# Fused attention and feed-forward: the feed-forward step regrouped from 256 tokens x 256 inner units to 512 tokens x 128 inner units, with the order of all engines written out

## The chip, the cores and the metric

The kernel runs on one core of a Trainium2 chip. The metric is the time of one execution in device microseconds (us); smaller is better. A profiled execution has a span as well, from the first to the last recorded instruction, which is a little shorter than its time.

## The reference

Two parts run one behind the other. The first is a sparse attention over 4 batches x 8 heads x 768 tokens x 64 dimensions. Each query sees the 31 keys nearest to it and 24 summaries, one for each block of 32 keys; a key summary is a maximum over its block, a value summary a mean:

```python
k_sum = k.reshape(B, H, nb, block, D).max(axis=3)
v_sum = v.reshape(B, H, nb, block, D).mean(axis=3)
mask_l = np.abs(pos[:, None] - pos[None, :]) < window
scores_s = scale * np.einsum('bhsd,bhnd->bhsn', q, k_sum) + np.log(block)
scores_all = np.concatenate([np.where(mask_l, scores_l, -1e9), scores_s], axis=-1)
a = softmax(scores_all)
x = np.matmul(a, np.concatenate([v, v_sum], axis=2))
```

The second is a feed-forward layer on the 3072 tokens x 512 channels that result, with 2048 inner units and the function Mish between two matrix products:

```python
h = x @ w_in
g = h * np.tanh(np.log1p(np.exp(h)))
out = g @ w_out
```

The two weight matrices are held as 64-bit floating-point numbers.

## The kernel before

**Work and tiles.** The 3072 tokens are cut into 12 chunks of 256 (c = 0 to 11), three to a batch. A chunk's attention has four units, one for each pair of heads (hp). A unit goes through: `att_load` (DMAs of queries with keys `qk` and of values `vw`; for a new batch also all keys `ks`, whose block maxima `km` DVE takes, and all values `vsum`, whose block sums `vq` DVE takes and whose means go back through a small DMA `vm<-vq` and from there into `vw<-vm`); `att_scores` (matmuls `sc` on PE, four masked row minima on DVE, line 261, four exponentials on ACT, line 266, the reciprocal of the sum on DVE, the scaling of `pr` on POOL, line 271); `att_transpose` (`pt_ps` on PE, copy `pt` on ACT); `att_values` (`x_ps` on PE, then the split of the result into a rounded part `xh` on ACT and a rest `xl` on DVE).

**Two-part numbers.** PE multiplies in a rounded 32-bit format, so each factor is split into a high and a low part and each product is made of three matmuls: high by high, low by high, high by low.

**Feed-forward.** The 2048 inner units are 16 blocks of 128 (fc). A step of `ff_in` takes one chunk and two blocks: 2 blocks x 4 channel blocks x 3 = 24 matmuls with 256 columns (line 313) into one bank `ph`. `ff_act` makes Mish on ACT (line 321), the high part `gh` (ACT for the first two chunks, DVE behind them, line 325) and the low part `gl` on DVE (line 326). `ff_out` adds the step into two output tiles `po` with 12 matmuls of 512 columns (line 340), two steps later. Eight steps make a chunk, 96 steps the kernel.

**Weights.** There are 32 weight blocks of 128 x 512 numbers, 16 of `w_in` and 16 of `w_out`. `load_weight` brings one in by a DMA of 512 KB into one of three staging buffers and converts it: two integer operations on DVE (lines 116, 117), a scaled copy on ACT (119), a clamp and a merge on DVE (120, 122), the high part by ACT (124), the low part by POOL (125). The converted blocks stay for the whole run.

**Order.** The list of steps runs chunks 0 and 1 beside each other, chunk 1 four steps behind. A dictionary `at` gives the turns at which the attention units of later chunks are put in. The program is then handed to a scheduler that works from a model of the times and sets the order on each engine anew; so the order on an engine isn't the one written. Each engine, and SP's queue of DMA issues, runs its own list strictly in that order and waits on semaphores.

Of the kernel before, what the change touches and what calls it, by code (L numbers as in the profile page):

```python
# [20 lines left out]
P = 128  # L21
# [15 lines left out]
NP_ = NFC // 2  # L37
EARLY = 10
NR = (S - CH) // P
LEAD = 4  # L40
AHEAD = 3
# [14 lines left out]
def fused_kernel(ctx: ExitStack, tc: tile.TileContext, q0, qk, kt, v0, vw, vs, w_in, w_out, out):  # L56
# [5 lines left out]
    xp = ctx.enter_context(tc.tile_pool(name="xp", bufs=3))  # L62
# [44 lines left out]
    def load_weight(src, hi, lo, name):  # L107
        t = stage.tile([P, WP], I64, tag="stage", name=name)
        nc.sync.dma_start(t, src)
        words = t.bitcast(U32).rearrange("p (f two) -> p f two", two=2)  # L110
        low, high = words[:, :, 0], words[:, :, 1]
        f = ff.tile([P, WP], F32, tag="f", name=f"{name}_f", bufs=3)
        x = ff.tile([P, WP], U32, tag="x", name=f"{name}_x", bufs=2)
        u = f.bitcast(U32)

# [3 lines left out]
        nc.scalar.activation(f, high.bitcast(F32), AF.Copy, scale=2.0 ** -OFFSET)  # L119
# [6 lines left out]

    def load_weights(n):
# [4 lines left out]
    weights = [(w, 2 * fp + j) for fp in range(NP_) for w in range(2) for j in range(2)]  # L132

# [101 lines left out]
    def att_psum(c, name):  # L235

        pool, tag = (ps_o, "o") if c == 0 else (ps_a, "a")
        return pool.tile([P, 512], F32, tag=tag, name=name)

    def att_scores(c, hp):  # L240
# [24 lines left out]
        for s in range(NQ):  # L265
            nc.scalar.activation(pr[:, s, :], pr[:, s, :], AF.Exp, scale=-1.0, bias=nm[:, s:s + 1],  # L266
                                 accum_out=sm[:, s:s + 1])
        rs = small.tile([P, NQ], F32, tag="rs", name=f"rs{c}_{hp}")
        nc.vector.tensor_scalar_add(rs, sm, 1e-9)
        nc.vector.reciprocal(rs, rs)  # L270
        nc.gpsimd.tensor_mul(pr, pr, rs.unsqueeze(2).broadcast_to([P, NQ, KA]))  # L271
        u["p"] = pr

    def att_transpose(c, hp):
        u = units[c, hp]
        ps = att_psum(c, f"pt_ps{c}_{hp}")
# [6 lines left out]
    def att_values(c, hp):  # L283
        u = units.pop((c, hp))
        if c not in xs:
            xs[c] = (xp.tile([P, HP, CH], F32R, tag="xh", name=f"xh{c}"),
                     xp.tile([P, HP, CH], F32R, tag="xl", name=f"xl{c}"))
        xh, xl = xs[c]
# [7 lines left out]
        nc.scalar.copy(xh[:, hp, :], ps[:, :CH])  # L296
        nc.vector.tensor_sub(xl[:, hp, :], ps[:, :CH], xh[:, hp, :].bitcast(F32))  # L297
# [5 lines left out]
    def ff_in(c, fp):  # L303
        i = c, fp
        xh, xl = xs[c]

        pool, tag = (ps_a, "a") if c == NCH - 1 and fp in (NP_ - 1, NP_ - 3) else (ps_h, "h")
        ph = pool.tile([P, 2, CH], F32, tag=tag, name=f"ph{c}_{fp}")
        for j in range(2):
            wh, wl = (weight(0, part, 2 * fp + j) for part in range(2))  # L310
            for cc in range(NCC):
                for n, (w, x) in enumerate(((wh, xh), (wh, xl), (wl, xh))):
                    nc.tensor.matmul(ph[:, j, :], w[:, cc * P:(cc + 1) * P], x[:, cc, :],  # L313
                                     start=(cc == 0 and n == 0), stop=(cc == NCC - 1 and n == 2))
        st[i] = {"h": ph.rearrange("p j t -> p (j t)")}

    def ff_act(c, fp):

        s = st[c, fp]
        g = ff.tile([P, 2 * CH], F32, tag="g", name=f"g{c}_{fp}", bufs=3)  # L320
        nc.scalar.activation(g, s["h"], AF.Mish)  # L321
        gh = ff.tile([P, 2 * CH], F32R, tag="gh", name=f"gh{c}_{fp}", bufs=3)
        gl = ff.tile([P, 2 * CH], F32R, tag="gl", name=f"gl{c}_{fp}", bufs=3)

        (nc.scalar.copy if c < 2 else nc.vector.tensor_copy)(gh, g)  # L325
        nc.vector.tensor_sub(gl, g, gh.bitcast(F32))  # L326
        s["g"] = (gh, gl)

    def ff_out(c, fp):
        i = c, fp  # L330
        gh, gl = st.pop(i)["g"]
        if fp == 0:
            po[c] = [ps_o.tile([P, DM], F32, tag="o", name=f"po{c}_{t}") for t in range(CH // P)]
        for t in range(CH // P):
            for j in range(2):
                fc = 2 * fp + j
                tok = slice(j * CH + t * P, j * CH + (t + 1) * P)
                wh, wl = (weight(1, part, fc) for part in range(2))
                for n, (g, w) in enumerate(((gh, wh), (gl, wh), (gh, wl))):
                    nc.tensor.matmul(po[c][t], g[:, tok], w,  # L340
                                     start=(fc == 0 and n == 0), stop=(fc == NFC - 1 and n == 2))
        if fp == NP_ - 1:
            for t in range(CH // P):
                o = ff.tile([P, DM], F32, tag="o", name=f"o{c}_{t}")
                nc.scalar.copy(o, po[c][t])
                nc.sync.dma_start(out[c * CH + t * P:c * CH + (t + 1) * P, :], o)


    todo = [(c, hp) for c in range(NCH) for hp in range(HP)]

    steps = [(c, i - c * LEAD) for i in range(NP_ + LEAD) for c in range(2) if 0 <= i - c * LEAD < NP_]
    steps += [(c, fp) for c in range(2, NCH) for fp in range(NP_)]

# [22 lines left out]
    def turn(k, lag):  # L376

        return k + lag - (k >= len(steps) - AHEAD)

# [64 lines left out]
```

## Time and profile before

| what | value |
|---|---|
| median of 3 runs | 713.33 us (710.31 to 714.52) |
| the profiled execution: time | 712.24 us |
| its span | 710.5 us |
| mean granted PE clock | 0.976 |
| PE busy | 672.8 us, 95% |
| ACT busy | 354.2 us, 50% |
| DVE busy | 301.1 us, 42% |
| POOL busy | 111.5 us, 16% |

Matmuls overlap one another, so the mean length of one says little; what counts is the distance from one start to the next. On DVE and ACT, too, an instruction starts a little (about 0.08 us) before its forerunner's recorded end. In rows of the timeline the columns are: start in us, length in us, engine, line, operation, output<-inputs, shapes, count, and in brackets how long the engine had stood idle and what ended that.

### The profile page before, as it was taken

To read this page: it belongs to the slowest core of one execution; us is meant where nothing else is said; L and a number is where in the kernel's file an instruction comes from. 1 tells how busy PE (TensorE), PEld (TensorE's weight loads), DVE (VectorE), ACT (ScalarE), POOL (GpSimd) and SP (SyncE) were. 2 spreads that over 40 slices of the span, in tenths; PEclk is the share of its full clock that TensorE was granted. 3 is DMA by queue.
4 is the path that set the end of the run, shared out by engine and by line. 5 is a ranking of instruction groups with operands and counts; after the bars stand their busy time and mean duration, and the time that the engine had idled before them with its cause. 6 is when DMAs were issued, how large, how long until landed. Compare 5 with 4: busy or idle time off the path is not lost.

```text
span 710.5 us, 12644 instructions
## 1 busy us (share of the span) xinstructions
PE 672.8 (95%) x4960; PEld 603.6 (85%) x4960; DVE 301.1 (42%) x872; ACT 354.2 (50%) x776; POOL 111.5 (16%) x151
## 2 busy tenths in 40 slices
PE   4978788799999999999999999999999999999998
PEld 3767677688898998998998998998998998998996
DVE  4899989952322334443223233222222322322211
ACT  2767755544556644644644644644644644644110
POOL 3454554301010010010100100100100100010000
PEclk9969899899999999999999999999999999999999
DMA  9876655772221323531311311311311311300000
GB/s 276 239 235 204 184 171 155 216 230 88 88 71 44 111 56 104 161 89 43 116 43 43 116 43 44 117 44 43 116 43 43 117 43 44 115 15 1 30 1 30
DMA packets 30683, 70.56 MB, mean 99 GB/s; under 512 B 4768, under 2 KB 9504, under 8 KB 30624
## 3 DMA queue, kind: packets, MB, share of 16 engines
q1 hardware_dynamic: 30624, 69.76, 32.2%
q8 instruction: 39, 0.64, 0.4%
q14 instruction: 20, 0.16, 0.1%
HBM read 61.15 MB, written 6.29 MB: 95 GB/s over the span
## 4 chain that ended last, share of the span: by engine, by line
PE 79%; DVE 11%; DMA 4%; issue 2%; ACT 2%; SPq 0%; POOL 0%; DVEq 0%; POOLq 0%
PE ph L313 34%; PE po L340 33%; PE sc L246 6%; PE x_ps L295 3%; DVE w_x L116 3%; PE pt_ps L278 2%; DVE w_x L117 2%; DVE w_f L122 2%; DMA ks<-kt 1%; DMA vsum<-vs 1%; DMA vw<-vw 1%; DVE w_f L120 1%; ACT pr L266 1%; DVE gl L326 1%; DVE vq L196 1%
## 5 line engine op out<-in xcount | busy, mean ns | idle before, releaser
L313 PE MATMUL ph<-xh,w_early_in_hi 128*128 128x256 f32 x480 | 138.7, 291 | 3.2 <-ACT w_early_in_hi L124 2.4
L313 PE MATMUL ph<-xh,w_early_in_lo 128*128 128x256 f32 x480 | 139.1, 291 | 2.2 <-POOL w_early_in_lo L125 2.2
L313 PE MATMUL ph<-xl,w_early_in_hi 128*128 128x256 f32 x480 | 138.9, 290 | 1.2 <-DVE xl L297 1.2
L325 DVE CAST gh<-g 128x512 fp32r<-128x512 f32 x80 | 34.3, 429 | 209.3 <-ACT g L321 196.6
L271 POOL TENSOR_TENSOR pr<-pr,rs 128x480 f32<-128x480 f32 x48 | 49.0, 1021 | 348.2 <-DVE rs L270 309.7
L313 PEld LDWEIGHTS ph<-xh,w_early_in_hi 128*128 128x128 f32 x480 | 93.9, 196 | 7.1 <-ACT w_early_in_hi L124 3.2
L313 PEld LDWEIGHTS ph<-xl,w_early_in_hi 128*128 128x128 f32 x480 | 93.8, 196 | 3.9 <-DVE xl L297 1.7
L313 PEld LDWEIGHTS ph<-xh,w_early_in_lo 128*128 128x128 f32 x480 | 93.9, 196 | 3.2 <-POOL w_early_in_lo L125 2.6
L340 PE MATMUL po<-w_early_out_hi,gh 128*128 128x512 f32 x240 | 94.3, 396 | 2.5 <-ACT gh L325 2.5
L340 PE MATMUL po<-w_early_out_hi,gl 128*128 128x512 f32 x240 | 95.6, 398 | 0.0
L340 PE MATMUL po<-w_early_out_lo,gh 128*128 128x512 f32 x240 | 95.0, 396 | 0.0
L321 ACT ACTIVATE g<-ph 128x512 f32<-128x512 f32 x96 | 57.4, 598 | 67.0 <-PE ph L313 66.5
L313 PE MATMUL ph<-xh,w_late_in_hi 128*128 128x256 f32 x288 | 82.5, 287 | 0.1
L313 PE MATMUL ph<-xh,w_late_in_lo 128*128 128x256 f32 x288 | 81.9, 284 | 0.1
L313 PE MATMUL ph<-xl,w_late_in_hi 128*128 128x256 f32 x288 | 81.1, 282 | 0.0
L266 ACT ACTIVATE pr<-pr,nm 128x120 f32<-128x120 f32 x192 | 73.7, 385 | 5.8 <-DVE nm L261 5.3
L321 ACT ACT_TABLE_LOAD x44 | 56.5, 1283 | 38.7 <-PE ph L313 38.3
L326 DVE TENSOR_TENSOR gl<-g,gh 128x512 fp32r<-128x512 f32 x96 | 70.7, 736 | 8.1 <-ACT gh L325 5.5
L296 ACT CAST xh<-x_ps 128x256 fp32r<-128x256 f32 x48 | 17.9, 372 | 100.7 <-PE x_ps L295 100.7
L280 ACT COPY pt<-pt_ps 120x512 f32<-120x512 f32 x48 | 28.1, 586 | 71.9 <-PE pt_ps L278 71.5
L266 ACT ACT_TABLE_LOAD x43 | 55.2, 1283 | 8.4 <-DVE nm L261 7.8
L340 PE MATMUL po<-w_late_out_hi,gl 128*128 128x512 f32 x144 | 56.7, 394 | 1.6 <-DVE gl L326 1.6
(75 smaller groups left out, 1149.9 us busy)
## 6 DMA issues: line engine op xcount, KB each, us to landing
qk<-qk SPq DMA_DIRECT2D x44, 496.0 KB
vw<-vw SPq DMA_DIRECT2D x48, 192.0 KB
w<-w_in SPq DMA_DIRECT2D x16, 512.0 KB
w<-w_out SPq DMA_DIRECT2D x16, 512.0 KB
ks<-kt SPq DMA_DIRECT2D x16, 384.0 KB
out<-o SPq DMA_DIRECT2D x24, 256.0 KB
vsum<-vs SPq DMA_DIRECT2D x12, 384.0 KB
vw<-vm SPq DMA_DIRECT2D x44, 48.0 KB
```

Of the source, the lines that this page charges most:

```text
L116: nc.vector.tensor_scalar(out=x, in0=low, scalar1=29, scalar2=None, op0=ALU.logical_shift_right)
L246: nc.tensor.matmul(ps[:, s * KA:(s + 1) * KA], u["qk"][:, s, 0:P], u["qk"][:, s, P:], start=True, stop=True)
L266: nc.scalar.activation(pr[:, s, :], pr[:, s, :], AF.Exp, scale=-1.0, bias=nm[:, s:s + 1], accum_out=sm[:, s:s + 1])
L271: nc.gpsimd.tensor_mul(pr, pr, rs.unsqueeze(2).broadcast_to([P, NQ, KA]))
L280: nc.scalar.copy(pt.rearrange("p s q -> p (s q)"), ps[:KA, :])
L295: nc.tensor.matmul(x, u["v"][:, s, d], pt, start=True, stop=True)
L296: nc.scalar.copy(xh[:, hp, :], ps[:, :CH])
L313: nc.tensor.matmul(ph[:, j, :], w[:, cc * P:(cc + 1) * P], x[:, cc, :], start=(cc == 0 and n == 0), stop=(cc == NCC - 1 and n == 2))
L321: nc.scalar.activation(g, s["h"], AF.Mish)
L325: (nc.scalar.copy if c < 2 else nc.vector.tensor_copy)(gh, g)
L326: nc.vector.tensor_sub(gl, g, gh.bitcast(F32))
L340: nc.tensor.matmul(po[c][t], g[:, tok], w, start=(fc == 0 and n == 0), stop=(fc == NFC - 1 and n == 2))
```

## The change

**Feed-forward steps.** Two chunks make a group g of 512 tokens. A step is now a group with one block of 128 inner units: `ff_in` 4 x 3 = 12 matmuls of 512 columns, `ff_out` 4 output tiles x 3 = 12 matmuls of 512 columns. There are 6 groups x 16 = 96 steps. The first step needs the attention of both chunks 0 and 1 (all channels, 512 tokens). The high part is now `ah`, the low part `al`, made in `ff_split`.

**Order.** Up to the first step the scheduler still sets the order, from a longer written list. From the first step on, everything stands within `tc.manual_schedule()`, and each engine takes the order in which the loop writes it. Within turn i that order is: `ff_in(i)`, Mish of i, values of the unit of turn i-2, scores of this turn's unit with the DMAs of keys, the DMAs of values, two weight blocks, the split of i, the sums of this turn's unit, `ff_out(i-2)`, the transposes of the unit of turn i-1. Chunks 2 and 3 have their eight units at turns 6 to 13, one each; later groups have one unit at every second turn.

**Weights in two halves.** `load_weight` begins a block (DMA, ACT's scaled copy, DVE's lines 117 and 118); `finish_weight` does the rest (126, 128, 130 on ACT, 131 on POOL) while the next block has been begun. Ten blocks are begun ahead of the first step, two at each of turns 0 to 10. Blocks come one `w_out`, one `w_in` in turn.

**Buffers.** Mish outputs, both halves of a weight and the outputs share one tag with 6 buffers; x has 2 instead of 3.

```diff
-NP_ = NFC // 2
+CG = 2
+TG = CG * CH
+NG = NCH // CG
-LEAD = 4
-AHEAD = 3
-    ff = ctx.enter_context(tc.tile_pool(name="ff", bufs=2))
+    ff = ctx.enter_context(tc.tile_pool(name="ff", bufs=6))
...
     def load_weights(n):
-        for w, fc in weights[:n]:
-            load_weight((w_in, w_out)[w][fc], weight(w, 0, fc), weight(w, 1, fc), f"w{w}_{fc}")
-        del weights[:n]
+        for _ in range(n):
+            if weights:
+                begun.append(load_weight(*weights.pop(0)))
+            if len(begun) > 1 or not weights and begun:
+                finish_weight(*begun.pop(0))
...
+    def ff_in(g, fc):
+        xh, xl = xs[g]
+        ph = ps_h.tile([P, TG], F32, tag="h", name=f"ph{g}_{fc}")
+        wh, wl = (weight(0, part, fc) for part in range(2))
+        for cc in range(NCC):
+            for n, (w, x) in enumerate(((wh, xh), (wh, xl), (wl, xh))):
+                nc.tensor.matmul(ph, w[:, cc * P:(cc + 1) * P], x[:, cc, :],
+                                 start=(cc == 0 and n == 0), stop=(cc == NCC - 1 and n == 2))
...
+        (nc.scalar.copy if g == 0 else nc.vector.tensor_copy)(ah, a)
+        nc.vector.tensor_sub(al, a, ah.bitcast(F32))
...
+    begin_with("K0 K1 S0 K2 V0 S1 W1 T0 K3 V1 S2 A0 T1 V2 S3 W1 A1 T2 V3 A2 T3 l0 W1 A3")
...
+    begin_with("l1 s0 W2 t0 s1 l2 W1 a0 t1 s2 W2 l3 a1 t2 s3 W1 a2 t3 l4 W1 a3 k5 v5")
...
+        at[(g - 1) * NFC + (2 * u - 1 if g > 1 else NFC - CG * HP - 2 + u)] = c, hp
...
+    with tc.manual_schedule():
+        for i in range(len(steps) + 2):
+            if i < len(steps):
+                ff_in(*steps[i])
+                ff_act(*steps[i])
+            if i - 2 in at:
+                att_values(*at[i - 2])
+            if i in at:
+                att_scores(*at[i])
+                if unit := next(keys, None):
+                    att_load_keys(*unit)
+            if i - 2 in at and (unit := next(values, None)):
+                att_load_values(*unit)
+            load_weights(2)
+            if i < len(steps):
+                ff_split(*steps[i])
+            if i in at:
+                att_normalize(*at[i])
+            if i >= 2:
+                ff_out(*steps[i - 2])
+            if i - 1 in at:
+                att_transpose(*at[i - 1])
```

**Three places of the new order.** A name such as w1_12 is block 12 of matrix 1 (`w_out`; matrix 0 is `w_in`), qk3_0 is pair 0 of chunk 3, al0_1 is group 0, step 1; the last number tells a tile from others.

On DVE, before, in the middle of the conversions (chunks 0 and 1):

```order
L120 TENSOR_SCALAR w1_11_f_1088<-w1_11_f_1088 128x512
L116 TENSOR_SCALAR w0_12_x_1143<-w0_12_1140 128x512
L122 SCALAR_TENSOR_TENSOR w1_11_f_1088<-w1_11_f_1088,w1_11_x_1089 128x512
L120 TENSOR_SCALAR w0_12_f_1142<-w0_12_f_1142 128x512
L117 SCALAR_TENSOR_TENSOR w0_12_x_1143<-w0_12_1140,w0_12_x_1143 128x512
L116 TENSOR_SCALAR w0_13_x_1154<-w0_13_1151 128x512
L122 SCALAR_TENSOR_TENSOR w0_12_f_1142<-w0_12_f_1142,w0_12_x_1143 128x512
```

On DVE, now, turn 0 from its second block on and the beginning of turn 1:

```order
L117 TENSOR_SCALAR w0_6_x_752<-w0_6_749 128x512
L118 SCALAR_TENSOR_TENSOR w0_6_x_752<-w0_6_749,w0_6_x_752 128x512
L126 TENSOR_SCALAR w1_4_f_740<-w1_4_f_740 128x512
L128 SCALAR_TENSOR_TENSOR w1_4_f_740<-w1_4_f_740,w1_4_x_741 128x512
L344 TENSOR_TENSOR al0_0_737<-a0_0_734,ah0_0_736 128x512
L117 TENSOR_SCALAR w1_5_x_782<-w1_5_779 128x512
L118 SCALAR_TENSOR_TENSOR w1_5_x_782<-w1_5_779,w1_5_x_782 128x512
```

The low part al of a step now stands directly behind the merge (L128) of the turn's second weight block and ahead of everything of the next turn, where before the low part (`gl`) stood wherever the scheduler had put it between conversions.

On ACT a turn now stands as: Mish, scaled copy and high part of one block, scaled copy and high part of the next, then the high part ah. So ah waits, by ACT's order, for the merge of the weight block ahead of it on DVE, and al on DVE for ah.

On SP's queue, before, the last eight weight blocks are issued in one piece:

```order
L109 DMA w0_12_1140<-w_in 128x512
L109 DMA w0_13_1151<-w_in 128x512
L109 DMA w1_12_1231<-w_out 128x512
L109 DMA w1_13_1242<-w_out 128x512
L109 DMA w0_14_1298<-w_in 128x512
L109 DMA w0_15_1309<-w_in 128x512
L109 DMA w1_14_1409<-w_out 128x512
L109 DMA w1_15_1420<-w_out 128x512
```

On SP's queue, now, turn 8:

```order
L222 DMA qk3_0_1228<-qk 128x992
L235 DMA vw2_2_1231<-vw 96x512
L239 DMA vw2_2_1231<-vm0_2_309 24x4x128
L111 DMA w1_12_1234<-w_out 128x512
L111 DMA w0_14_1245<-w_in 128x512
```

On SP's queue, now, turn 10, the last with weights:

```order
L222 DMA qk3_2_1430<-qk 128x992
L205 DMA vsum1_0_1434<-vs 96x1024
L209 DMA vm1_0_1433<-vq1_0_1436 24x4x32
L235 DMA vw3_0_1440<-vw 96x512
L239 DMA vw3_0_1440<-vm1_0_1433 24x4x128
L111 DMA w1_14_1443<-w_out 128x512
L111 DMA w1_15_1454<-w_out 128x512
```

The weight blocks of turns 8 to 10 are now issued behind attention DMAs of the same turn: qk3_0 needs the buffer that this turn's scores (chunk 2, pair 2) read, vw2_2 the buffer that this turn's values read, vm1_0 the result of DVE's sum of this turn.

More of the change, by code (lines that the diff above doesn't have):

```diff
@@ L118, in load_weight, with finish_weight @@
                                        op0=ALU.bitwise_and, op1=ALU.bitwise_or)
-        nc.scalar.activation(f, high.bitcast(F32), AF.Copy, scale=2.0 ** -OFFSET)
+        return w, fc, f, x
+    def finish_weight(w, fc, f, x):
+        u = f.bitcast(U32)
+        hi, lo = (weight(w, part, fc) for part in range(2))
         nc.vector.tensor_scalar(out=f, in0=f, scalar1=-_as_f32(F32_MAX), scalar2=_as_f32(F32_MAX),
@@ L284, in att_values @@
         u = units.pop((c, hp))
[L285 to L288, printed above, removed]
+        g, half = divmod(c, CG)
+        if g not in xs:
+            xs[g] = (xp.tile([P, HP, TG], F32R, tag="xh", name=f"xh{g}"),
+                     xp.tile([P, HP, TG], F32R, tag="xl", name=f"xl{g}"))
+        xh, xl = (x[:, hp, half * CH:(half + 1) * CH] for x in xs[g])
         ps = att_psum(c, f"x_ps{c}_{hp}")
@@ L295, in att_values @@
                 nc.tensor.matmul(x, u["v"][:, s, d], pt, start=True, stop=True)
-        nc.scalar.copy(xh[:, hp, :], ps[:, :CH])
-        nc.vector.tensor_sub(xl[:, hp, :], ps[:, :CH], xh[:, hp, :].bitcast(F32))
+        nc.scalar.copy(xh, ps[:, :CH])
+        nc.vector.tensor_sub(xl, ps[:, :CH], xh.bitcast(F32))
     st = {}
     po = {}
[L303 to L346, printed above, removed]
@@ new lines, in ff_split, with ff_out @@
+    def ff_split(g, fc):
+        a, ah, al = st[g, fc]
+        (nc.scalar.copy if g == 0 else nc.vector.tensor_copy)(ah, a)
+        nc.vector.tensor_sub(al, a, ah.bitcast(F32))
+    def ff_out(g, fc):
+        _, ah, al = st.pop((g, fc))
+        if fc == 0:
+            po[g] = [ps_o.tile([P, DM], F32, tag="o", name=f"po{g}_{t}") for t in range(TG // P)]
+        wh, wl = (weight(1, part, fc) for part in range(2))
+        for t in range(TG // P):
+            tok = slice(t * P, (t + 1) * P)
+            for n, (a, w) in enumerate(((ah, wh), (al, wh), (ah, wl))):
+                nc.tensor.matmul(po[g][t], a[:, tok], w,
+                                 start=(fc == 0 and n == 0), stop=(fc == NFC - 1 and n == 2))
+            if fc == NFC - 1:
+                o = ff.tile([P, DM], F32, tag="t", name=f"o{g}_{t}")
+                (nc.vector.tensor_copy if t % 2 else nc.scalar.copy)(o, po[g][t])
+                nc.sync.dma_start(out[g * TG + t * P:g * TG + (t + 1) * P, :], o)
@@ L376, in turn @@
-    def turn(k, lag):
-        return k + lag - (k >= len(steps) - AHEAD)
-    loaded = HP + 1
-    for i in range(len(steps) + 2):
-        parts = at.get(i, ())
-        now = [x for k, x in enumerate(steps) if turn(k, 0) == i]
-        for x in now:
-            ff_in(*x)
-        for x in now:
-            ff_act(*x)
-        for f, c, hp in parts:
-            if f is not att_transpose:
-                f(c, hp)
-                if f is att_scores and loaded < len(todo):
-                    att_load(*todo[loaded])
-                    loaded += 1
-        load_weights(4 if i < LEAD else 2)
-        if i >= 2:
-            ff_out(*steps[i - 2])
-        for f, c, hp in parts:
-            if f is att_transpose:
-                f(c, hp)
+    for c, hp in todo[CG * HP:]:
+        g, half = divmod(c, CG)
+        u = half * HP + hp
+        at[(g - 1) * NFC + (2 * u - 1 if g > 1 else NFC - CG * HP - 2 + u)] = c, hp
```

59 lines of the change are left out of this document (35 added, 24 removed).

## The prediction

> **What bounds the kernel now.** I read the page first: the span, the slices, the shares of the chain.
>
> ```profile
> span 710.5 us, 12644 instructions
> PE   4978788799999999999999999999999999999998
> DVE  4899989952322334443223233222222322322211
> PEclk9969899899999999999999999999999999999999
> PE 79%; DVE 11%; DMA 4%; issue 2%; ACT 2%; SPq 0%; POOL 0%; DVEq 0%; POOLq 0%
> ```
>
> A slice is 710.5 / 40 = 17.8 us. Up to the eighth (142 us) DVE is mostly at 8 or 9 tenths and PE at 7 or 8; behind the ninth PE is full to the end. So there are two stages: one in which weights are converted, and one in which only matmuls count. The windows and the chain of waits put numbers on both (columns of a window: length, then busy time and instructions of PE, PEld, DVE, ACT, POOL, then PE's clock, DMA share, GB/s).
>
> ```profile
> 40.00:60.00 20.00, 16.82 (x119) 14.81 (x120) 19.49 (x45) 14.16 (x37) 11.86 (x11) 0.68 0.66 212
> 404.17:457.54 53.37, 53.37 (x403) 48.35 (x402) 17.47 (x64) 25.31 (x58) 4.85 (x8) 1.00 0.22 68
> ```
>
> ```profile
> 146.78 3.45 DMA vsum<-vs
> 151.88 6.05 DMA vsum<-vs
> 404.17 2.86 PE ph L313 x24
> 407.03 2.75 PE po L340 x12
> 696.07 10.98 PE po L340 x48
> ```
>
> In the second stage a chunk is 53.37 us of unbroken PE: 8 steps of 2.86 + 2.75 = 5.61, and 53.37 - 44.9 = 8.5 for four attention units, 2.1 each. In the first stage DVE is busy 19.49 of 20 us at 40 to 60. The last long wait that is not PE's is the sum's transfer, ending at 157.9.
>
> **The change: matmuls.** 24 matmuls of 256 columns take 2.86, 12 of 512 take 2.75, so a step of `ff_in` should fall to 2.75: 96 x 0.11 = 10.6 us less PE work in all. The rows are of the same operands' types and the same clock of 1.00. The Trainium skill, "TensorE: Matmul & The Clock Gate", Back-to-back issue gap, gives N / 2.4 + 2.5 ns for one matmul taken alone, which is 109 and 216 ns; the trace's spacing, 119 and 229 ns, is wider at both. By that formula a pair saves only 2.6 ns, and the total below would come out about 7 us higher.
>
> **The change: the way to the first step.** The first step now needs chunks 0 and 1 whole. The listing of the order shows nine merges of weights (L128) and five reciprocals (L287) on DVE up to the one of chunk 1's first unit, and then hardly any conversions beside units 1 to 3. Before, DVE had done as much when this merge, the ninth, had ended:
>
> ```profile
> 51.78 0.68 DVE L122 SCALAR_TENSOR_TENSOR w_f<-w_f,w_x 128x512 uint32<-128x512 uint32 x1
> ```
>
> So 52 us. Behind it stand three units one after the other, since PE's order puts each unit's scores behind the transposes of the one before. The links of that chain:
>
> ```profile
> 25.19 0.65 PE L278 MATMUL pt_ps<-ident,pr 128*120 128x128 f32 x4 [1.18 <-POOL pr L271]
> 34.84 0.69 PE L295 MATMUL x_ps<-pt,vw 120*64 120x64 f32 x16
> 40.95 1.90 PE L246 MATMUL sc<-qk 128*128 128x120 f32 x8
> 402.07 1.15 PE L246 MATMUL sc<-qk 128*128 128x120 f32 x8
> ```
>
> ```profile
> 131.38 0.40 ACT L266 ACTIVATE pr<-pr,nm 128x120 f32<-128x120 f32 x1 [0.92 <-DVE nm L261]
> ...
> 132.81 0.19 ACT L266 ACTIVATION_READ_ACCUMULATOR pr<-pr,nm 128x1 f32 x1
> ```
>
> ```profile
> 26.71 0.99 POOL L271 TENSOR_TENSOR pr<-pr,rs 128x480 f32<-128x480 f32 x1 [1.57 <-DVE rs L270]
> ```
>
> ```profile
> L261 DVE CUSTOM_DVE_ANT_0 pr<-sc,base 128x120 f32<-128x120 f32 x160 | 36.3, 277 | 8.4 <-PE sc L246 8.1 <-issue 0.4
> L296 ACT CAST xh<-x_ps 128x256 fp32r<-128x256 f32 x48 | 17.9, 372 | 100.7 <-PE x_ps L295 100.7
> L280 ACT COPY pt<-pt_ps 120x512 f32<-120x512 f32 x48 | 28.1, 586 | 71.9 <-PE pt_ps L278 71.5
> ```
>
> Scores 1.15 to 1.90 (the clock was 0.68 in that window), first minimum 0.28 and a hand-over, four exponentials 1.6 (131.38 to 133.00), two small sums on DVE 0.4, POOL 1.0, transposes 0.65, hand-overs about 0.4: 5.5 to 6.9 a unit, and I take 6.1. Ahead of them come the first unit's POOL, transposes and copy, 2.8 with hand-overs; behind them the last copy, values, xh and xl, 2.1. So 52 + 2.8 + 3 x 6.1 + 2.1 = 75 us to the first step. Low end 66 (DVE keeps its 19.49 of 20 from the start: 39 us of work in 43, and short units), high end 79 (long units, DVE late).
>
> **The change: turns 0 to 5.** Here each turn converts two blocks and DVE takes al last. The rows are of before, same shapes:
>
> ```profile
> 101.61 0.68 DVE L326 TENSOR_TENSOR gl<-g,gh 128x512 fp32r<-128x512 f32 x1
> 102.21 0.68 DVE L122 SCALAR_TENSOR_TENSOR w_f<-w_f,w_x 128x512 uint32<-128x512 uint32 x1
> 102.81 0.68 DVE L117 SCALAR_TENSOR_TENSOR w_x<-w,w_x 128x512 uint32<-128x512 uint32 x1
> 103.42 0.41 DVE L120 TENSOR_SCALAR w_f<-w_f 128x512 f32<-128x512 f32 x1
> 103.75 1.51 DVE L116 TENSOR_SCALAR w_x<-w 128x512 uint32<-128x512 uint32 x1
> 105.19 0.68 DVE L122 SCALAR_TENSOR_TENSOR w_f<-w_f,w_x 128x512 uint32<-128x512 uint32 x1
> ...
> 116.24 1.78 DVE L326 TENSOR_TENSOR gl<-g,gh 128x512 fp32r<-128x512 f32 x1
> ```
>
> ```profile
> 103.62 1.36 POOL L125 TENSOR_TENSOR w_late_out_lo<-w_f,w_late_out_hi 128x512 fp32r<-128x512 f32 x1 [2.22 <-ACT w_late_out_hi L124]
> 116.12 1.35 POOL L125 TENSOR_TENSOR w_late_out_lo<-w_f,w_late_out_hi 128x512 fp32r<-128x512 f32 x1 [2.22 <-ACT w_late_out_hi L124]
> ```
>
> ```profile
> 80.92 0.62 ACT L124 CAST w_early_in_hi<-w_f 128x512 fp32r<-128x512 f32 x1
> 81.45 0.61 ACT L325 CAST gh<-g 128x512 fp32r<-128x512 f32 x1
> ```
>
> By starts, a long DVE operation takes 0.60 and a short one 0.34, so the four of a block 1.88. One that meets POOL's subtraction takes 1.44 instead of 0.34 (103.75 to 105.19), 1.1 more, so such a block 2.98. In a turn, counted from its second merge: ACT makes that block's high part (0.53 to the next start) and then ah (0.61), so al can start at 1.2; what is queued behind it on DVE is all of the next turn's weight work. POOL meanwhile makes the low part, 0.7 to 2.1, so al ends at 2.6, as in the row at 116.24. The next block ends its four at 4.5, the second, with POOL in its way, at 7.5. PE would need 2.75 + 2.75 = 5.5, so it waits for al. Six turns of 7.5 are 45 us; bounds 6.6 (al clear of POOL, 0.6 instead of 1.4) and 8.5 (both blocks meet POOL), 40 to 51.
>
> **Turns 6 and 7.** Scores add four minima (0.8) to DVE in turn 6, and in turn 7 the sums and POOL's scaling as well (0.4, and 0.7 of POOL in DVE's way): 8.3 + 9.4 = 17.7, bounds 16 to 19.
>
> **Turns 8 and 9.** The transfers decide here. In SP's listing the two weight blocks stand behind `qk`, which needs a buffer that the turn's scores free, and behind `vw`, which needs one that the turn's values free. Before, such a wait was there too, but no weights behind it:
>
> ```profile
> SPq L224 <- PE x_ps L295: 281.1, 33, 12.4
> ```
>
> ```profile
> 139.94 0.81 SPq L198 DMA_DIRECT2D vm<-vq  x1
> ...
> 149.54 0.84 SPq L228 DMA_DIRECT2D vw<-vm  x1
> ```
>
> The values wait for the copy pt, which on ACT stands behind ah of the turn before, and that stands behind that turn's second high part. From ah's end: pt copy 0.6, values to 2.4, scores to 3.45, `qk`, `vw`, and 0.84 for `vw<-vm`, so the first weight block is issued at 5.1 to 5.4. The page has no landing time for 512 KB; the sum's transfer, 384 KB, took 3.45 and 6.05. I take 4.5: the blocks are there at 9.6, where DVE would want the first at 6. Both are converted, 4.5 to 5.4 with merges and high part: 15 us a turn, 30 for two. Bounds 11 (the 3.45, no collision) and 17 (the 6.05, both collide).
>
> **Turn 10** has three waits in a row on SP: `qk` for scores, `vm` for DVE's sum, `vw<-vm` for `vm`; only then the last two blocks. In the row below DVE gets its buffer back from the small transfer at 142.94, 3.0 after the issue at 139.94; the sum itself takes 1.22.
>
> ```profile
> 142.94 1.22 DVE L196 TENSOR_REDUCE vq<-vsum 96x32 f32<-96x1024 f32 x1 [0.85 <-DMA vm<-vq]
> ```
>
> That is 15 + 1.2 + 0.2 for the mean + 3.0 + 0.84 for `vw<-vm` = 20.2, and 1.8, one clean block, for the sum's place in DVE's list: 22. Bounds: 12, if the sum's data were there long before and DVE reaches it early; 27, if `vsum` lands in 6.05 first. **Turn 11** takes 10 (8.2 to 11), the last conversions without new ones, and 3.5 more reach turn 12's scores.
>
> **The rest is PE.** Left then are 86 `ff_out` and 83 `ff_in`, 169 x 2.75 = 464.8, and 34 units' worth of attention, 34 x 2.1 = 71.4: 536.2. The end costs what it costs now, 710.5 - (696.07 + 10.98) = 3.5. The output copies and their transfers lie beside PE but for the last; DVE's share, 17.47 of 53.37, and ACT's leave room there for every order, so buffers and the written order cost nothing; without that room a turn with attention, 7.6, would show it.
>
> **Sum:** 75 + 45 + 17.7 + 30 + 22 + 10 + 3.5 + 536.2 + 3.5 = 742.9, against the span of 710.5. The profiled execution's time was 712.24, 1.7 more than its span: 744.6, so 745 us. That execution stands 1.1 under the median of the three runs, 713.33, well inside their spread of 4.2, so nothing is added for it. All low ends give 66 + 40 + 16 + 22 + 12 + 8.2 + 3.5 + 539.7 + 1.7 = 709, all high ends 79 + 51 + 19 + 34 + 27 + 11 + 3.5 + 539.7 + 1.7 = 766.
>
> One more price lies in ACT's switches between Mish and the exponential:
>
> ```profile
> 52.93 1.28 ACT L321 ACT_TABLE_LOAD   x1
> 54.22 0.60 ACT L321 ACTIVATE g<-ph 128x512 f32<-128x512 f32 x1
> ```
>
> Mish starts 1.29 after the load began: the load and nothing more. The Trainium skill, "ScalarE: Activation LUTs", What ACT_TABLE_LOAD costs, adds about 1.38 us of drain to each switch, which these rows don't show. By it turns 6 to 11, two switches each, would be up to 12 x 1.38 = 17 us longer and the time up to 761.
>
> **Rivals.** *Weights arrive in time.* Turns 8 to 11 then go by their low bounds, near turn 7's 9.4: 11 + 11 + 12 + 8.5 = 42.5 in place of 15 + 15 + 22 + 10 = 62, so 19.5 less: 725 us. For it: three staging buffers, and a transfer of 3.45. Against it: SP's order.
>
> *Conversion keeps up* (the other side, faster). If DVE's turn is no longer than PE's, 5.5 or 7.6 with attention, PE is bound from the first step on: 75 + 96 x 5.5 + 40 x 2.1 + 3.5 + 1.7 = 692 us. It decides at a DVE turn of 5.5: DVE's bare work is 2 x 1.88 + 0.6 = 4.4 without POOL, 4.4 + 2 x 1.1 = 6.6 with both subtractions in its way. For it: before, DVE did run 19.49 of 20 full, and the first stage there had the same work. Against it: al's wait for ah, which no order of other work fills now.
>
> *The losses are all at their low ends*, 709 us, no change. That the change doesn't do what it says is excluded by the listing, in which every engine has the written order from the first step on.
>
> **How the numbers follow.** Forecast, 726 to 766: 0.58. Weights in time, about 725: 0.16. Conversion keeps up, 690 to 705: 0.15. Low ends, within 0.5% of 713.33 (about what a measurement of this kernel can tell from no change; 709.8 to 716.9): 0.06. Over 766: 0.05. Leaving out the last and the fast case, 0.20, the range is 707 to 766. Faster 0.15, same 0.06, slower 0.58 + 0.16 + 0.05 = 0.79.
>
> **What would show it.** In the changed profile: `ff_in` as x12 of 2.75; the first step at 75; starts of al 7.5 apart in turns 0 to 5, each idle for ACT's ah; in turns 8 to 10 DVE's L117 waiting for a DMA of `w`, and SP's queue waiting for PE ahead of weight blocks; sc of turn 12 at 203; PE full behind it. The prediction is wrong if PE is full before 150, or if DVE never waits for `w`.

## The result, and the profile after

The changed kernel takes 771.9 us (median; 771.61 to 773.79) against 713.24 us (710.31 to 714.52): the ratio is 1.083, 95% interval 1.080 to 1.087. The profiled execution has a span of 770.3 us. Slower was forecast, and 745 us with a range to 766; the loss is 58.7 us where 31 were foreseen.

From the page after, the same five lines that were read of before:

```profile
span 770.3 us, 10267 instructions
PE   6636886745499999999899999989999999999997
DVE  4971887644533323244532232354323232221211
PEclk9755899786599999999999999999999999999999
PE 63%; DVE 16%; DMA 14%; ACT 3%; issue 2%; POOL 1%; SPq 1%; POOLq 0%; DVEq 0%
```

A slice is now 19.3 us. PE isn't full before the twelfth slice (212 us; before, the ninth, 142 us), and two dips of one slice stand behind that, at the 20th (366 us) and the 27th (501). DVE is less busy in the first stage than before, not more: nothing has become the bound by being busy. The share of transfers in the chain has gone from 4% to 14%. The low clock figures stand where PE waits; from 240 us on the clock is 1.00, as it was before. Two windows, first the one in which the first step's attention is made, then turns 8 and 9:

```profile
40.00:60.00 20.00, 6.95 (x39) 6.01 (x40) 12.25 (x35) 8.14 (x25) 8.47 (x8) 0.50 0.58 187
160.00:200.00 40.00, 19.58 (x104) 16.12 (x104) 18.48 (x44) 15.29 (x33) 7.07 (x8) 0.71 0.37 121
```

At 40 to 60 DVE had 19.49 of 20 us before and has 12.25 now. At 160 to 200 no engine is busy for half of the time.

From the chain of waits after, the start:

```profile
50.77 0.99 POOL pr L288
...
61.21 3.40 DMA qk<-qk
...
69.16 3.92 DMA qk<-qk
...
78.28 0.35 DVE w_x L117
```

The first unit of chunk 1 is scaled at 50.8 and turn 0 begins at 78. Then turns 0 and 1 (the rows of the second are those of the first, 8.2 us later):

```profile
84.95 1.38 DVE al L344
86.35 0.44 DVE w_x L117
...
88.60 0.44 DVE w_x L117
...
89.76 1.45 DVE w_f L126
...
92.48 0.62 ACT ah L343
93.12 1.37 DVE al L344
```

And the ends of turns 7 to 11, with the weight transfers that turns 8, 9 and 10 waited for:

```profile
143.45 0.26 ACT ah L343
...
148.32 4.29 DMA w<-w_out
...
158.73 0.61 ACT ah L343
...
164.92 6.86 DMA w<-w_out
...
177.89 0.61 ACT ah L343
...
191.46 3.56 DMA w<-w_out
...
201.13 0.61 ACT ah L343
...
213.36 0.52 ACT ah L343
...
215.10 1.09 PE sc L257 x8
```

Behind them PE is full, but for the turns in which a new batch's values come in. The scores of every second turn, with the transfer that stands between them in the chain:

```profile
330.41 1.09 PE sc L257 x8
...
331.93 4.24 DMA vsum<-vs
...
339.14 1.00 POOL pr L288
...
344.22 1.09 PE sc L257 x8
...
345.75 5.08 DMA vsum<-vs
...
358.89 1.10 PE sc L257 x8
...
387.82 1.08 PE sc L257 x8
...
400.97 1.08 PE sc L257 x8
```

The last pair, 13.15 apart, is a clean one. The four such pairs of turns from 330.41 to 387.82 take 57.41 in place of 52.6: 4.8 us lost here, and 5.5 in the same way from 493 to 551.

The terms of the sum against these rows (us; a turn from one ah's end to the next):

| term | forecast | measured |
|---|---|---|
| first step | 75 | 77.9 |
| turns 0 to 5 | 45 | 48 (7.0 for turn 0, then 8.2 each) |
| turns 6 and 7 | 17.7 | 17.8 |
| turns 8 and 9 | 30 | 34.8 (15.6 and 19.2) |
| turn 10 | 22 | 23.2 |
| turn 11 | 10 | 12.1 |
| to the scores of turn 12 | 3.5 | 1.2 |
| the rest with its end | 539.7 | 555.2 |
| span | 742.9 | 770.3 |

### The profile page after: what moved, and what is told of

Its sections match the earlier page's. It is cut to its first block, busy times and chain, and to the rows that moved or that the text cites. A ratio compares the mean times of both kernels' runs of the same rounds, so it can differ in the third digit from the quotient of the medians.

```text
span 770.3 us, 10267 instructions
## 1 busy us (share of the span) xinstructions
PE 674.9 (88%) x3808; PEld 546.0 (71%) x3808; DVE 313.7 (41%) x884; ACT 340.3 (44%) x758; POOL 109.8 (14%) x151
## 4 chain that ended last, share of the span: by engine, by line
PE 63%; DVE 16%; DMA 14%; ACT 3%; issue 2%; POOL 1%; SPq 1%; POOLq 0%; DVEq 0%
PE ph L328 26%; PE po L354 24%; DMA vsum<-vs 7%; PE sc L257 6%; PE x_ps L314 3%; DMA w<-w_out 3%; DVE w_f L126 3%; DVE w_x L118 3%; PE pt_ps L296 3%; DVE w_f L128 3%; DVE w_x L117 2%; DVE al L344 2%; DVE vq L207 2%; POOL pr L288 1%; DMA qk<-qk 1%
## 5 line engine op out<-in xcount | busy, mean ns | idle before, releaser
L335 ACT ACTIVATE a<-ph 128x512 f32<-128x512 f32 x96 | 57.3, 597 | 191.9 <-PE ph L328 191.7
L354 PE MATMUL po<-w_early_out_hi,ah 128*128 128x512 f32 x240 | 98.9, 412 | 4.9 <-ACT ah L343 3.4
L328 PE MATMUL ph<-xh,w_early_in_hi 128*128 128x512 f32 x240 | 98.9, 412 | 3.2 <-ACT xh L315 3.2
L354 PE MATMUL po<-w_early_out_hi,al 128*128 128x512 f32 x240 | 96.3, 401 | 4.4 <-DVE al L344 4.4
L328 PE MATMUL ph<-xl,w_early_in_hi 128*128 128x512 f32 x240 | 96.0, 400 | 0.0
L328 PE MATMUL ph<-xh,w_early_in_lo 128*128 128x512 f32 x240 | 95.9, 400 | 0.0
L354 PE MATMUL po<-w_early_out_lo,ah 128*128 128x512 f32 x240 | 95.5, 398 | 0.0
L344 DVE TENSOR_TENSOR al<-a,ah 128x512 fp32r<-128x512 f32 x96 | 79.7, 830 | 19.0 <-ACT ah L343 16.2
L277 ACT ACTIVATE pr<-pr,nm 128x120 f32<-128x120 f32 x192 | 73.6, 384 | 14.3 <-DVE nm L272 13.8
L335 ACT ACT_TABLE_LOAD x41 | 52.6, 1283 | 32.8 <-issue 19.5
L328 PE MATMUL ph<-xh,w_late_in_hi 128*128 128x512 f32 x144 | 58.1, 404 | 0.0
L354 PE MATMUL po<-w_late_out_hi,ah 128*128 128x512 f32 x144 | 57.9, 402 | 0.0
L354 PEld LDWEIGHTS po<-w_early_out_hi,ah 128*128 128x128 f32 x240 | 46.5, 194 | 15.6 <-ACT ah L343 4.6
```

What stands on the lines that cost most here:

```text
L328: nc.tensor.matmul(ph, w[:, cc * P:(cc + 1) * P], x[:, cc, :], start=(cc == 0 and n == 0), stop=(cc == NCC - 1 and n == 2))
L335: nc.scalar.activation(a, st[g, fc], AF.Mish)
L344: nc.vector.tensor_sub(al, a, ah.bitcast(F32))
L354: nc.tensor.matmul(po[g][t], a[:, tok], w, start=(fc == 0 and n == 0), stop=(fc == NFC - 1 and n == 2))
```

## The experiments

The theory after the result: the time goes into lists that are kept strictly in order, in four places. They are the start that needs two chunks, al behind weights, weights behind attention's transfers on SP, and al, ah and the reciprocal behind the sum of a new batch. The rivals: a slower PE clock; DVE's own work; the new step itself. Each run is set against the kernel before on the same chip (714.2, 713.8, 712.2, 714.1, 714.2 and 713.7 us in the six groups below), and the changed kernel's 771.9 is the base unless another is named. The kernel before differs by 2 us between these groups, so a difference of that size between two runs says little. The first step begins at 76.2 to 80.7 us in the profiled executions of runs that share its start, so a single profile can be some us early or late from the start on.

**1. The sums of a new batch last in the turn, from turn 12 on.**

```diff
-            if i - 2 in at and (unit := next(values, None)):
-                att_load_values(*unit)
+            unit = next(values, None) if i - 2 in at else None
+            if unit and i < LATE:
+                att_load_values(*unit)
             load_weights(2)
...
                 att_normalize(*at[i])
+            if unit and i >= LATE:
+                att_load_values(*unit)
```

> The values' loads with DVE's sum of a new batch (vsum, L207) moved behind the split and the sums of the turn, from turn 12 on; the work is the same. Theory: from turn 12 on the time over the forecast is the wait of DVE for the transfer vsum, ahead of ah, al and the reciprocal: 4.8 us for each of two later batches (scores 13.8, 14.7, 15.0, 13.9 us apart instead of 13.15) and 7.9 us in turns 12 and 13. So 17 us less, 755 us, and no idle time of DVE for vsum on the chain of waits behind 235 us. Rival, a lower PE clock (mean 0.936 against 0.976): no change, 772.

Measured: 762.8 us (757.98 to 764.79), ratio 1.068 [1.064, 1.073]; 9 less, where 17 were expected. From turn 12's scores to the span's end it is 544.7 us in the profile (211.6 to 756.3) against 555.2. The scores between which the changed kernel lost its first 4.8 us:

```profile
325.92 1.08 PE sc L258 x8
...
379.27 1.08 PE sc L258 x8
```

That is 53.35 for four pairs of turns, 52.6 when clean, in place of 57.41. The four pairs from 484.54 to 537.15 take 52.6 in place of 58.1. So the wait for vsum in the later batches was what I took it for, 10 us; the 7.9 for turns 12 and 13 was wrong. From the scores of turn 12 to those of turn 15 this run takes 22.2 us (211.62 to 233.83), and PE is busy for 28.37 of the 28.4 us from 211.6 to 240. The changed kernel took 23.3 there: 1.1 were lost, not 7.9. The clock isn't the cause: it was 1.00 in these stretches in both.

**2. Weight transfers at the head of the turn.**

```diff
         for i in range(len(steps) + 2):
+            for b in weights[:2]:
+                fetched[b] = fetch_weight(*b)
             if i < len(steps):
                 ff_in(*steps[i])
```

> The two weight transfers of a turn issued at its head, ahead of its attention transfers; DVE, ACT and POOL keep their order. Theory: turns 8, 9 and 10 (15.6, 19.2 and 23.2 us from the end of one ah to the next) are long because the transfers stand behind the attention's on SP; ahead of them, turns 8 and 9 fall to 10 or 11, turn 10 to about 17, where the sum stays in the way: 19 us less, 753. Rival, DVE and ACT bound these turns through their own lists: under 5 us less, 767 or more.

Measured: 757.3 us, ratio 1.062 [1.060, 1.064]; 14.6 less. From the chain, the same ends of turns:

```profile
142.53 0.61 ACT ah L349
...
153.93 0.61 ACT ah L349
...
166.04 0.61 ACT ah L349
...
182.39 0.61 ACT ah L349
```

Turns 8, 9 and 10 are 11.4, 12.1 and 16.4 us for 15.6, 19.2 and 23.2. No transfer of weights is left in the chain from 120 to 200 us, and turn 10 waits for vsum (3.48 at 171.47), as expected. Turn 12's scores come 18.4 us earlier (196.65); about 4 of these are given back, since the turns that load a new batch take longer here: 25.2 us for 23.3 from turn 12's scores to turn 15's, and 60.1 for 57.4 over the four pairs of the next batch. Why they do wasn't followed up.

**3. The split ahead of the weights.**

```diff
+            if i < len(steps):
+                ff_split(*steps[i])
             load_weights(2)
-            if i < len(steps):
-                ff_split(*steps[i])
```

> ah and al of a step made ahead of the turn's two weight blocks instead of behind them. Theory: al's wait for ah, which waits for the second merge, is 1.2 us of each 8.2 us turn; without it turns 0 to 5 fall to 6.9, and 6 and 7 by as much: 10 us less, 762. Rival, DVE's own work with POOL in its way fills the turn: turns stay at 7.7 or more, under 4 us less.

Measured: 781.4 us, ratio 1.094 [1.091, 1.098]; 9.5 more. The theory fell as it was put. Turns stayed above 7.7 us, as the rival said, but neither foresaw that the time would rise. The chain of turn 1:

```profile
88.13 0.70 DVE w_f L128
...
88.85 0.62 ACT w_early_out_hi L130
89.47 0.51 ACT a L335
...
90.00 0.63 ACT ah L343
...
90.66 0.03 DVE al L344
...
97.93 0.63 ACT ah L343
```

A turn is 7.93 in place of 8.2. al no longer waits for a merge of its own turn; but on ACT the next Mish now stands behind the high part of the turn before, and ah behind Mish, so that al begins 1.83 us behind the merge's end (88.83 to 90.66) where it had begun 1.19 behind it (91.93 to 93.12). That al no longer meets POOL (0.7 us for 1.37) makes up for this and a little more, 0.3 a turn. The wait went to another list, and in the turns with attention the exponentials stand in it too (in the chain from 143.21, ahead of ah at 144.53): turn 12's scores came at 222.8, not 215.1.

**4. The scheduler throughout.** `with tc.manual_schedule():` becomes `if True:`; steps, halves and buffers are the new ones.

> The new steps, halves and buffers, but the scheduler sets the order of all engines throughout, as in the kernel before. Theory: the loss is the written order, not the new steps: 700 to 740 us, with weights converted by 160 us. Rival, the new step itself costs it, because the first one needs two chunks: the first step not before 70 us and 745 us or more.

Measured: 755.1 us (750.24 to 760.89), ratio 1.059 [1.053, 1.065]. The theory's range is missed, and the figures are those of the rival, 745 us or more with a first step not before 70: steps 0 and 1 are made in pieces beside the attention, and the first 12 matmuls of a step that run on end begin at 85.3. But this run doesn't price the written order, since the scheduler's order has losses of its own, in another place. In windows of PE, 185.0 of the first 240 us are busy, where the changed kernel has 157.5; in the 450 us behind that, 20.5 are idle, where it has 8.6.

**5. The split between the halves of two blocks.**

```diff
             if weights:
                 begun.append(load_weight(*weights.pop(0)))
+            if middle and _ == n - 1:
+                middle()
             if len(begun) > 1 or not weights and begun:
                 finish_weight(*begun.pop(0))
...
-            load_weights(2)
-            if i < len(steps):
-                ff_split(*steps[i])
+            load_weights(2, (lambda: ff_split(*steps[i])) if i < len(steps) else None)
```

> The split of a step put between the beginning of the turn's second block and the finish of the one before it, so that ah on ACT waits for one merge less and DVE has two operations to do while ah is made. Theory after the run with the split first: turns 0 to 5 of 8.2 us are 5.6 of two blocks on DVE, 1.4 of al and 1.2 of waiting for ACT's high parts; with the wait covered they fall to 6.9 or 7.0, and turns 6 and 7 by as much: 762 us. Rival, each place of the split only moves the wait to another engine's list, as when it stood first: turns of 7.8 or more, 768 us or more.

Measured: 767.6 us (765.53 to 771.01), ratio 1.077 [1.071, 1.083]; 4.3 less, where 10 were expected. al of two turns, from the timeline of DVE:

```profile
91.34 1.12 DVE L346 TENSOR_TENSOR al<-a,ah 128x512 fp32r<-128x512 f32 x1 [0.59 <-ACT ah L345]
...
98.66 1.10 DVE L346 TENSOR_TENSOR al<-a,ah 128x512 fp32r<-128x512 f32 x1 [0.59 <-ACT ah L345]
```

A turn is 7.3 us, between both expectations. Half of the wait for ah is gone (0.59 left of 1.2): ah now stands behind one high part and a scaled copy. In this execution the first step began 1.9 us later (79.7), and ah of turn 5 ended 5.4 earlier all the same (120.5).

**6. The three orders together**, with the sums last in every turn.

> All three changes of order together: split between the halves, weight transfers at the head of the turn, sums of the values last in every turn. Theory, the prices add: 15 for the transfers, 9 for the sums, 9 for the split, and 5 more in turns 10 and 11, where the sum no longer stands ahead of weights: 771.9 - 38 = 734 us, between 728 and 740. Rival, what is taken from one wait is given back to another: 745 us or more.

Measured: 738.7 us, ratio 1.037 [1.032, 1.042]; 33.2 less, in the range, near its upper end. The prices add: 9.1, 14.6 and 4.3 alone make 28, and 5 more were expected of turns 10 and 11. Turn 10 did fall to 12.1 us (16.4 in run 2), while turn 11 took 13.8 (12.3 there).

**7. Five blocks ahead of the first step instead of ten**, on the base of run 6 (738.7). Five of the `W1` and `W2` in the two written lists of the beginning are taken out.

> As the run with the three orders, with five weight blocks begun ahead of the first step instead of ten, and the other five in later turns. Theory: DVE's conversions set when chunk 1's first unit is normalised (50.7 us), so 5 x 3.1 = 15 us less work brings the first full step from 78 to 63 or 66 us; three more turns with conversions give back 6 to 9: 4 to 8 us below the run with the three orders. Rival, the attention chain of chunks 0 and 1 with its transfers sets the start: the first step stays at 74 or later, and the time is 5 us or more above that run.

Measured: 745.6 us, ratio 1.044 [1.038, 1.051]; 7 more. The first step came at 70.7 instead of 80.7: 10 us earlier (5 to 10 against the other runs with ten blocks), a third to two thirds of DVE's work that was taken away, so conversions do set a part of the start. But the price at the other end was 17 by these two executions, not 6 to 9: turns 11, 12 and 13 then hold conversions and a new batch at once and take 18.0, 15.9 and 14.4 us (ah at 164.0, 182.0, 197.9 and 212.3). Both expectations miss, the theory on the price, the rival on the start.

**8. Small transfers one turn later**, on the base of run 6.

```diff
-        nc.sync.dma_start(vm, vq)
+        small_dma.append((vm, vq))
...
             if i in at:
                 att_normalize(*at[i])
+            flush()
```

> As the run with the three orders, with the small transfers of the means (vm, and vw from vm) issued one turn later, behind the next turn's keys. Theory: what is left of the loss in turns 12 to 14 there (190 to 216 us from the scores of turn 12 to those of turn 15, against 6.6 + 13.2 = 20 when PE sets it) is a loop on SP of sum, small transfer, next keys, next sum; without it 6 us less than 738.7, 730 to 734. Rival, the landing of vsum itself (4.7) sets these turns: within 2 us of 738.7.

Measured: 733.1 us, ratio 1.031 [1.027, 1.034]; 5.6 less, in the range. Only a part of that is shown to come from the loop on SP: in the profiles turns 12 to 14 went from 26.1 to 24.2 us, and the step from turn 11's scores to turn 12's from 11.0 to 9.3, while the profiled execution also began its first step 4.5 us earlier (76.2 for 80.7). The orders tried so far have given back 38.8 of the 58.7 us.

**9. Transposes at the head of the next turn**, on the base of run 8, up to turn 13.

> As the run before this one in the list, with the transposes of a unit at the head of the next turn instead of its end, up to turn 13. Theory: turns 8 to 11 took 11.9 us there because the copy pt stands behind ah on ACT, the values, scores and minima behind it, and the weight blocks behind the minima on DVE; with the copy at the head they fall to 9 or 10: 8 to 10 us less than the run with the small transfers deferred, 721 to 726, still not below 714. Rival, the transfers of keys (ks, km) and DVE's own work set these turns: under 3 us less.

Measured: 751.8 us, ratio 1.056 [1.054, 1.058]; 18.7 more than run 8. Both expectations fell, since neither foresaw a rise. From the chain of turn 8, and what PE waited for in all:

```profile
154.46 1.59 POOL w_late_in_lo L138
...
158.39 1.26 POOL w_late_out_lo L138
159.65 0.95 POOL pr L305
160.65 1.11 PE pt_ps L313 x4
```

```profile
PE pt_ps L313 <- POOL pr L305: 52.8, 10, 13.9
```

The exponentials end at 151.8. The small sum stands behind the two weight blocks and al on DVE and starts at 157.6; the scaling of `pr`, ready at 158.0, then stands behind a low part on POOL that ends at 159.65. From 120 to 215 us PE waited 9.5 us for it with the transposes at the end of the turn (run 8), all at one time. At the head of the next turn it waits 34.5 us, and ah and the weights wait behind PE: 15 us a turn for 11.9.

**10 and 11. The start written too, with blocks beside the units of chunk 1**, on the base of run 8.

```diff
-    begin_with("l1 s0 W2 t0 s1 l2 W1 a0 t1 s2 W2 l3 a1 t2 s3 W1 a2 t3 l4 W1 a3 k5 v5")
+    with tc.manual_schedule():
+        begin_with("l1 s0 W1 t0 s1 l2 W1 a0 W1 t1 s2 W1 l3 a1 W1 t2 s3 W1 a2 W1 t3 l4 W1 a3 k5 v5")
```

> As the run with the small transfers deferred, but the order of chunk 1's attention is written too, with one or two weight blocks beside each of its units; ten blocks are done ahead of the first step as before, the eleventh begun. Theory: the start is late (78 us, here 80) because DVE first converts ten blocks and then idles through three units of chunk 1; with the blocks put into those gaps, units of 7 to 8 us begin at about 33 instead of 50 and the first step comes at 62 to 70: 717 to 725 us. Rival, the written order stretches a unit to 11 us by waits in ACT's and POOL's lists: first step at 76 or later, 730 us or more.

> The same with thirteen blocks begun ahead of the first step. Theory: the start comes about 5 us later than with eleven, and one turn of 12 us with weights becomes one of 7: within 4 us of that run. If it is 6 us or more lower, the turns with weights and attention in one are the dearer place for a block; if 6 us or more higher, the start is.

Measured: 746.3 us, ratio 1.048 [1.042, 1.054], with the first step at 89, and 747.7 us, 1.049 [1.044, 1.054], with it at 99. The rival was right, and short: a unit took 14 to 18 us in the first and 16 to 22 in the second. From one of them, between the transposes at 57.58 and those at 71.76 in the first run:

```profile
66.55 0.43 DVE L124 TENSOR_SCALAR w_x<-w 128x512 uint32<-128x512 uint32 x1 [1.61 <-DMA w<-w_in]
...
68.69 0.16 DVE L303 TENSOR_SCALAR rs<-sm 128x4 f32<-128x4 f32 x1
```

```profile
69.50 1.26 POOL w_early_out_lo L138
```

The exponentials end at 62.5. The small sum `rs` stands behind two weight blocks on DVE, the second of which waits for its transfer, and starts only at 68.7: that is 6 us. The scaling of `pr`, ready at 69.1, then stands behind a low part on POOL that ends at 70.8. So most of the stretch is DVE's list, and the smaller part POOL's.

The second run's start is 10 us later, where 5 were expected, and its time only 1.4, within the 4 expected; so a block in a turn with attention costs about as much as one at the start.

**12. The scheduler through turn 13, the written order of run 8 behind it.**

```diff
+    for i in range(14):
+        one_turn(i)
     with tc.manual_schedule():
-        for i in range(len(steps) + 2):
+        for i in range(14, len(steps) + 2):
+            one_turn(i)
```

> As the run with the small transfers deferred (733.1), but the scheduler sets the order through turn 13, and the written order begins at turn 14. Theory: in the stage with conversions the scheduler fills ACT's, POOL's and SP's lists better (PE was busy for 185.0 us of the first 240 with it, 181.8 in the run with the small transfers deferred), and in the stage behind it the written order is better (PE idle 20 us behind 240 us with the scheduler, none there): 725 to 731 us. Above 714 all the same, since the first step needs two chunks. Rival, the idle time behind 240 us with the scheduler comes from the new steps and not from its order: 740 us or more.

Measured: 720.2 us, ratio 1.011 [1.007, 1.014]; 5 below the theory's range. So in the first stage the scheduler's order is worth 13 us against the best that I wrote, and behind turn 14 the written one is better than the scheduler's: of the 450 us behind 240, PE is idle for 0.4, where run 4 had 20.5. What is left, 6 us over the kernel before, has a place. PE's window from 40 to 80 us, here and in the kernel before (length, PE busy, clock, share and rate of transfers):

```profile
40.00:80.00 40.00, 19.57 (x131) 0.70 0.53 161
40.00:80.00 40.00, 31.49 (x216) 0.84 0.62 197
```

That is 11.9 us less of PE; from 80 to 240 us the two differ by 3.2 more. DVE is busy for 4.67 of the 20 us from 60 to 80, and was for all 20 before: the chain of chunk 1's units (transfers of `qk` of 3.75, 4.25 and 5.26 us in it) leaves it nothing to do.

**13. The kernel before with chunks 0 and 1 in step**, chunk 1's whole attention written ahead of the first step.

```diff
-LEAD = 4
+LEAD = 0
...
+    for hp in range(HP):
+        att_scores(1, hp)
+        att_load(*todo[loaded])
+        loaded += 1
+        load_weights(1)
+        att_transpose(1, hp)
+        att_values(1, hp)
```

> The kernel before, with its own steps of 256 tokens and its scheduler, but chunks 0 and 1 are run in step with each other (no lead of four steps), and the whole attention of chunk 1 is written ahead of the first step. Theory: a part of the loss is that two chunks' attention must be done before the matmuls can run on: 10 to 25 us more than before, 724 to 739 us. Rival, the new steps need not cost anything at the start, it is the order written from there on: within 5 us of 714.

Measured: 740.3 us, ratio 1.038 [1.033, 1.042]; 26 more than before, just over the theory's range. But the profile says that it isn't the same loss: PE has 13.76 of 40 us at 80 to 120, and DVE is full all through it, since the scheduler now put conversions ahead of what PE waits for.

```profile
80.00:120.00 40.00, 13.76 (x74) 0.50 0.62 201
```

It shows that a start with two chunks can cost 26 us with the old steps too. It doesn't show that it must.

**14. The old start and the new steps.** Chunks 0 and 1 run in steps of 256 tokens with chunk 1 four behind, under the scheduler; from chunk 2 on the steps are the new ones, from turn 14 on in the order of run 8.

```diff
+    steps = [(0, i - c * 4, c) for i in range(NFC // 2 + 4) for c in range(2) if 0 <= i - c * 4 < NFC // 2]
+    steps += [(g, fc) for g in range(1, NG) for fc in range(NFC)]
```

> Chunks 0 and 1 in the steps of the kernel before (256 tokens, 256 inner units, chunk 1 four steps behind), ordered by the scheduler; from chunk 2 on the new steps, and from turn 14 on the written order with its sums late and its small transfers deferred. Theory: the start that waits for two chunks is what the new steps cost, and the step of 512 columns saves 0.11 us; 80 such steps save 8.8 us: 704 to 709 us, faster than both kernels. Rival, the seam or the written order behind it costs as much as the steps save: 712 us or more.

Measured: 709.5 us (704.58 to 714.02), ratio 0.9957 [0.9926, 0.9987]. It is the only version that beats both kernels, by 0.4%, which the interval just tells from no change. In the profiled execution (704.58 us, at the low end of its spread) PE is busy 661.2 us against 672.8 before: 11.6 less, where 80 steps by 0.11 were 8.8. The start is back at DVE's old pace (19.32 of 20 us at 60 to 80). The expectation holds for that execution; the median is 0.5 above its upper end and below the rival's 712. The buffers, which were changed together with the steps, are those of the changed kernel here, so no loss of theirs shows.

## Why the prediction was wrong, step by step

- **The matmuls** were right: 12 of 512 columns take 2.76 (row below, one line for many), and 16 steps with eight units 8 x 13.15 = 105.2 us against 2 x 53.37 = 106.7 before. The other price given there, 2.6 ns saved for each pair of matmuls, doesn't fit: the spacing went from 2 x 119 to 230 ns, 8 ns less.

```profile
242.21 2.76 PE ph L328 x12
```

- **The first step** was right in size (77.9 for 75) and half right in its links. DVE's work ended when forecast (50.8 for 52). But the three units took 22.7 us from transposes to transposes (51.81 to 74.50) where I had 3 x 6.1 = 18.3: in the last two, transfers of keys of 3.40 and 3.92 us stand in the chain, behind which the scaling waits on POOL, and not the exponentials and small sums that I had put there. An earlier beginning hid a part of that, which was luck.
- **Turns 0 to 5** were right in their mechanism, and 1.88 us for a block was mis-sized: that is the pace at which each operation is followed by one that doesn't need its result. In the written order L118 stands behind L117 of the same block and L128 behind L126, and the four operations take 2.25 (86.35 to 88.60), with POOL in their way 3.35: 1.4 for al, 2.25, 3.35 and 1.2 of waiting for ah make 8.2 a turn, not 7.5.
- **Turns 8 to 11** were right in their mechanism (run 2 takes the weight transfers away and the turns fall to 11 and 12), and short by 8 us: the landings were 4.29 and 6.86 where 4.5 stood for both, from a landing's end to ah's end it took 6.7 (152.61 to 159.34) where 4.5 to 5.4 stood, by the same mis-sized blocks as in turns 0 to 5, and turn 11 held a second vsum. Turns 8 and 9 (34.8 for 34 at most) and turn 11 (12.1 for 11) passed even their high ends, by 2 us together.
- **The step that failed** is the last term: "DVE's share, 17.47 of 53.37, and ACT's leave room there for every order, so buffers and the written order cost nothing". Room in an engine says nothing of a wait in its list. In the turns that load a new batch the sum stands ahead of ah, al and the reciprocal: transfer, sum, split, reciprocal and scaling lie between the scores' end and the transposes, 331.50 to 340.14 with a landing of 4.24, and longer with 5.08; PE has 3 x 2.75 = 8.25 of other work for these 8.6. I had followed exactly this wait in turn 10 and not asked for it in the eight turns of that kind in the two later batches. It cost 10 us, and run 1 gives them back. The term as a whole was 15.5 us short: 10.3 in these eight turns, 1.1 in turns 12 to 14, and 4 in small misses of the PE sum itself, since run 1, with PE unbroken there but for half a us and the end, still takes 544.7 for 539.7. With no upper end for that term, a range made from all the others ended at 766.
- **Rival, conversion keeps up**: refuted; no turn up to 12 was bound by PE. **Rival, weights in time**: refuted by the rows of 148 to 195 us. **The longer switch of ACT's tables**: the load at 144.47 takes 1.28 in the chain and Mish starts at 145.77, so nothing was added at that switch, as at the one shown from before the change.
- **What the runs divide the loss into**: of 58.7 us, 39 are the order written from the first step on, shown by runs 1, 2, 5, 6 and 8; of the 20 left 13 more are order, shown by run 12, and the last 6 lie at the start, where run 14 with the old start loses none. In the profiled executions PE is idle for 15 us more of the span in run 12 than before (720.4 - 667.7 = 52.7 against 710.5 - 672.8 = 37.7), and the shorter matmuls pay a part of it back. Whether a start with two chunks must cost that, or only in the orders tried, stays open.

## What to carry to other kernels

An engine that is free half of the time can still hold up the one that is the bound: read a written order list by list, and for each instruction that waits ask what stands behind it. A wait that is taken out of one list can come up in another (runs 3, 9 and 10), so the loop through all lists has to be followed round, not one edge of it. And a larger step that saves PE time needs more of the input before it can begin; a start in small steps and the rest in large ones had both.

## What was not expected of the hardware

- In turns 0 to 7 of the changed kernel a DVE operation that needs the result of the one ahead (L118 behind L117, L128 behind L126) starts 0.03 or 0.04 us behind its end, in all 32 pairs; L126, which stands behind another block's L118, starts 0.08 or 0.09 before that one's end. Over the four operations that was 2.25 against 1.88 us. L117 behind L128 starts 0.03 late as well, though it is another block's; why, no run shows.
- A DVE operation that meets POOL's subtraction was stretched from 0.42 to 1.5 us in each of the turns 0 to 6 (in the chain 1.45 at 89.76, and its like 8.2 us later), always the clamp of the second block: the order written fixed the collision's place.
- The landing of the same 512 KB took 4.29, 6.86 and 3.56 us within 50 us. The queue had other transfers under way each time: in windows of 4.3, 6.9 and 3.7 us around these landings it moved 338, 297 and 237 GB/s, about 1.45, 2.05 and 0.88 MB in all.
